# Half tiles moved into the arm that repeats in float32: one branch arm less on the way to the end of an attention and mixture-of-experts kernel

## The chip, the cores and the metric

The kernel runs on one core of one Trainium2 chip. The metric is the time of one execution on the device, in microseconds, as the median of several runs. Lower is better.

## The reference

Attention with capped scores over 4 batches of 12 heads (448 tokens, head size 64), and then a mixture of 8 experts in which each of the 1792 tokens goes to the one expert whose embedding is nearest:

```python
scores = scale * np.matmul(q, k.transpose(0, 1, 3, 2))
scores = cap * np.tanh(scores / cap)
attn = softmax(scores)
x = np.matmul(attn, v)            # (4, 12, 448, 64) -> x: (1792, 768)
...
expert_idx = np.argmax(logits, axis=1)
gate_w = probs[np.arange(N), expert_idx]
for e in range(E):                # E = 8
    mask = expert_idx == e
    h = np.maximum(x[mask] @ w1[e], 0.0)        # w1[e]: 768 x 1024
    out[mask] = gate_w[mask, None] * (h @ w2[e])  # w2[e]: 1024 x 768
```

## The kernel before

The first half of the kernel computes the attention, chooses an expert for each token and counts the tokens of each. After that the experts are ordered by their counts. An expert's place in this order is its position, 0 to 7. Its tokens are taken in tiles of 128. Each weight matrix is split into two float16 halves (`split1`, `split2`), and a product is made of three float16 products. If a sum over the low halves shows that float16 was not enough, the whole mixture is repeated in float32 (`plain_tile`). `fine_sums` and `overflow` compute that test from `sums`: a matmul adds up a count, DVE writes `redo_i`, all engines load it into a register and branch on it (L1575, L1576).

For each position the program holds a number `code` in a register: twice the count of full tiles, plus one if a half tile is left. `position(p)` is nested: `position(p + 1)` stands inside the branch that `position(p)` takes for full tiles. Positions 1 to 4 (`WIDE`) take the leftovers of up to 32 tokens along with a full tile (`wide_tile`) and have no half tiles. From position 5 on there are two branches, one behind the other: `code == 1` runs a half tile (L1547), and `code > 1` runs full tiles and the next position (L1549). Where that second one isn't taken, its `Else` arm asks whether the next position has any tokens (L1555) and runs the half tiles that are left.

`chain(p)` runs the full tiles of one position, with a branch (L1526) ahead of each but the first. `foretell` writes a hint for a branch: it stands some time ahead of the branch and names it and its condition. It is put on TensorE, ScalarE, DVE and POOL, not on SyncE.

`tile_body` (through `any_tile`) is one tile. POOL first computes the tile's `gt` and `idx_out`. TensorE makes the hidden layer in two halves, ScalarE and DVE split each into `hh` and `hl`, and TensorE multiplies by `w2`. Behind the sixth of eight parts it transposes the next tile's `x_tile`, which ScalarE and DVE copy to `xh` and `xl` (`transpose_x`), and POOL scales the one after that (`scale_x`). Then DVE writes `yo`, POOL sends it with an indirect DMA (L677), and POOL gathers one more tile of tokens (L197, L198). The argument `nxt` says which; `False` leaves all of this preparation out. Functions in `hooks` run at numbered places of a tile; 0 to 11 are the steps of its first products.

POOL's program is one queue: indirect DMAs, scalings and the branches stand in order. At the end of the kernel POOL drains and then the engines meet.

Of the kernel before, what the change touches and what calls it, by code (L numbers as in the profile page):

```python
# [30 lines left out]
F32 = mybir.dt.float32  # L31
F32R = mybir.dt.float32r
F16 = mybir.dt.float16
I32 = mybir.dt.int32
AF = mybir.ActivationFunctionType
ALU = mybir.AluOpType
# [44 lines left out]
def attention_moe(ctx: ExitStack, tc: tile.TileContext, q, k, v, cap, emb, tau, w1, w2, qk_pairs, v_pairs, out):  # L81
# [1151 lines left out]
    def positions():  # L1233
# [17 lines left out]
        nc.vector.tensor_copy(pos_i, by_pos[0:1, 3:5, :])  # L1251

    def start_loads():
        for p in range(1, E):
            eid[p] = nc.values_load(
                pos_e[0:1, p : p + 1], engines=(mybir.EngineType.SP,), min_val=0, max_val=E - 1
            )
        for i in range(N1):
            load1(1, i)
        for f in range(N2):  # L1260
            load2(1, f)
# [220 lines left out]
    fine_s = work.tile([P, 1], F16, tag="fine_s", name="fine_s")  # L1482
    redo_i = work.tile([P, 1], I32, tag="redo_i", name="redo_i")

# [5 lines left out]

    def overflow():
        fp = tile_of("h", 0)
        nc.tensor.matmul(fp[:, 0:1], ones16, fine_s, start=True, stop=True)  # L1493
        nc.vector.tensor_scalar(redo_i, fp[:, 0:1], float(P * NF), None, op0=ALU.is_lt)  # L1494


    with tc.manual_schedule():
# [12 lines left out]
        def half_tile(p, hooks=()):  # L1510

            _, base = ends[p]
            any_tile(p, base, base + 3 if p < E - 1 else False, P // 2, hooks=hooks)

# [21 lines left out]
        def position(p):  # L1536
# [10 lines left out]
            with tc.If(code == 1):  # L1547
                half_tile(p, {0: [lambda: foretell(f"full{p}", code > 1)]})
            with tc.If(code > 1, label=f"full{p}") as arm:  # L1549
                chain(p)  # L1550
                position(p + 1)
            if p < E - 1:
                with arm.Else():

                    with tc.If(ends[p + 1][0] > 0):  # L1555
                        for n in range(p + 1, E):
                            with tc.If(ends[n][0] == 1):
                                for f, *a in todo_for(n):
                                    f(*a)
                                half_tile(n)  # L1560

# [9 lines left out]
        fine_sums()  # L1571
        overflow()


        redo = nc.values_load(redo_i[0:1, 0:1], min_val=0, max_val=1)  # L1575
        with tc.If(redo > 0):  # L1576

            nc.vector.tensor_scalar(pos_i[:, 0, :], pos_i[:, 0, :], 1, None, op0=ALU.add)
            nc.vector.tensor_scalar(pos_i[:, 0, :], pos_i[:, 0, :], 1, None, op0=ALU.logical_shift_right)
            nc.vector.tensor_tensor(pos_i[:, 0, 0:1], pos_i[:, 0, 0:1], first_i[0:1, 1:2], op=ALU.add)  # L1580
            nc.vector.memset(pos_i[:, 1, 0:1], 0)
            with tc.For_i(0, E, 1) as p:
                e = nc.values_load(
                    pos_e[0:1, bass.ds(p, 1)], engines=(mybir.EngineType.SP,), min_val=0, max_val=E - 1
                )
                for i in range(N1):
                    nc.sync.dma_start(raw1[i], w1_part(e, i))
                for f in range(N2):
                    nc.sync.dma_start(raw2[f], w2_part(e, f))
                n = nc.values_load(pos_i[0:1, 0, bass.ds(p, 1)], min_val=0, max_val=NT // P + 1)  # L1590
                base = nc.values_load(
                    pos_i[0:1, 1, bass.ds(p, 1)], engines=(mybir.EngineType.Pool,), min_val=0, max_val=TMAX
                )

                with tc.For_i(0, n, 1) as slot:
                    plain_tile(base + slot)
                plain_tile(p + TAIL0)

# [46 lines left out]
```

## Time and profile before

| | |
|---|---|
| median of 3 runs | 546.03 us (545.84 to 549.48) |
| profiled execution | 543.88 us |
| its span, first to last instruction | 542.1 us |
| TensorE busy in the span | 89% |
| DVE, ScalarE, POOL busy | 61%, 55%, 45% |
| mean granted TensorE clock | 0.963 |

Times are in microseconds from the start of the span, unless they are marked ns. The engines are PE (TensorE matmul), PEld (its weight loads), DVE, ACT (ScalarE), POOL and SP; a q behind the name means the sequencer of that engine. Branches, semaphore waits and register loads are the sequencer's work. They are not counted as busy and do not stand in the timeline, but the view of a source line lists them. There a row reads: line, engine, operation and its count, then the shortest, median and longest duration in ns, then the start of the first and of the last. A row of the timeline reads: start, duration, engine, line, operation, tile written and tiles read, shapes, count, and in brackets the idle time before it with what ended it. A row of the stretches gives the stretch, its length, the busy time and count of PE, PEld, DVE, ACT and POOL, the granted clock, the share of the DMA engines and GB/s. The page also lists two DMA queues of the kind "instruction", which carry the program's code to the engines.

### The profile page before, as it was taken

How to read it: one execution, taken by the hardware profiler on the slowest of the kernel's cores; microseconds unless marked ns; L12 is line 12 of the kernel's file. 1: busy time of each engine (PE TensorE's matmuls, PEld its weight loads, DVE VectorE, ACT ScalarE, POOL GpSimd, SP SyncE). 2: the span in 40 equal slices, each digit the busy share in tenths (PEclk: the TensorE clock that was granted, in tenths of full speed). 3: DMA queues.
4: the chain of work that ended last, by engine and by line, in shares of the span. 5: the costliest groups of instructions: out<-in, count | busy, mean ns of one | idle time of the engine just before them, and what ended most of it. 6: DMA issues, size and time to landing. Idle time of an engine off the chain costs nothing. (4 is left out here: it accounts for less than half of the span.)

```text
span 542.1 us, 11950 instructions
## 1 busy us (share of the span) xinstructions
PE 482.8 (89%) x4603; PEld 312.3 (58%) x4604; DVE 329.5 (61%) x712; ACT 300.5 (55%) x371; POOL 245.6 (45%) x294
## 2 busy tenths in 40 slices
PE   3999999999997979979698799999999999998970
PEld 1444444444443434347676578877887788777650
DVE  4876686868698679588719521771125812496710
ACT  3987789788978887926128210831115511567410
POOL 2567556564643454640136412843235623553531
PEclk9999999999999979989999799999999999998995
DMA  7433218331451540325299711491112931297921
GB/s 228 128 112 113 76 63 289 111 112 67 148 207 62 190 160 0 104 73 164 97 390 365 282 40 59 175 344 59 61 60 96 382 114 61 87 366 258 332 86 39
DMA packets 30595, 83.51 MB, mean 154 GB/s; under 512 B 7293, under 2 KB 7449, under 8 KB 30498
## 3 DMA queue, kind: packets, MB, share of 16 engines
q1 hardware_dynamic: 26354, 67.68, 35.7%
q0 software_dynamic: 2896, 13.00, 6.8%
q10 hardware_dynamic: 1248, 1.64, 0.9%
q8 instruction: 47, 0.77, 0.6%
q14 instruction: 50, 0.41, 0.2%
HBM read 69.91 MB, written 13.00 MB: 153 GB/s over the span
## 5 line engine op out<-in xcount | busy, mean ns | idle before, releaser
L780 ACT ACTIVATE prob<-s,icap 128x896 f32<-128x896 f32 x96 | 86.3, 904 | 24.7 <-PE s L774 16.7
L794 POOL TENSOR_TENSOR sums<-sums,prob 128x896 f32<-128x896 f32 x23 | 48.4, 2102 | 81.8 <-DVE sums L792 62.7
L231 PEld LDWEIGHTS <-h 128*128 128x128 f16 x1056 | 79.7, 99 | 7.4 <-issue 3.8
L784 ACT ACTIVATE prob<-prob,cap_b 128x896 f32<-128x896 f32 (+1 forms) x64 | 81.7, 1277 | 2.1
L231 PE MATMUL h<-xh,h 128*128 128x128 f16 (+1 forms) x480 | 78.7, 218 | 2.6 <-ACT x_tile L669 1.4
L231 PE MATMUL h<-xl,h 128*128 128x128 f16 (+1 forms) x480 | 78.8, 218 | 0.9 <-issue 0.9
L231 PE MATMUL h<-xh,l 128*128 128x128 f16 (+1 forms) x480 | 78.8, 218 | 0.5 <-issue 0.4
L811 PE MATMUL v<-prob,vb 128*64 128x448 f32 x288 | 72.2, 581 | 2.9 <-DVE xt L826 2.8
L800 POOL TENSOR_TENSOR sums<-sums,prob 64x448 f32<-64x448 f32 x47 | 64.6, 1375 | 3.6
L204 POOL TENSOR_TENSOR x_tile<-xg 128x768 f32<-128x768 f32 x17 | 25.3, 1489 | 83.8 <-PE xt L212 74.1
L231 PEld LDWEIGHTS <-l 128*128 128x128 f16 x528 | 51.8, 99 | 1.1 <-issue 1.1
L215 ACT CAST xh<-xt 128x384 f16<-128x384 f32 x32 | 13.9, 481 | 68.5 <-PE xt L212 60.5
L244 DVE SCALAR_TENSOR_TENSOR hl<-h,hh 128x512 f16<-128x512 f32 (+1 forms) x20 | 13.3, 664 | 62.6 <-ACT hh L243 62.6
L243 ACT ACTIVATE hh<-h 128x512 f16<-128x512 f32 (+1 forms) x20 | 11.5, 574 | 67.1 <-PE h L231 67.1
L774 PE MATMUL s<-hi 64*128 64x448 f32 x144 | 35.5, 484 | 14.1 <-DVE hi L756 11.8
L1388 PE MATMUL h<-xh,h 128*128 128x160 f16 x192 | 41.1, 237 | 5.1 <-ACTq L1526 2.6
L216 DVE TENSOR_TENSOR xl<-xt,xh 128x384 f16<-128x384 f32 x32 | 16.4, 551 | 46.3 <-ACT xh L215 46.2
L638 PEld LDWEIGHTS <-hh 128*128 128x128 f16 (+1 forms) x352 | 32.9, 100 | 19.4 <-issue 1.2
L222 DVE SCALAR_TENSOR_TENSOR l<-w1r,by_pos,h 128x1024 f16<-128x1024 f32 x30 | 37.7, 1305 | 9.8 <-ACT h L221 9.8
L774 PEld LDWEIGHTS s<-hi 64*128 64x128 f32 x144 | 14.4, 190 | 46.9 <-ACT prob L780 16.0
L1388 PE MATMUL h<-xh,l 128*128 128x160 f16 x192 | 41.1, 238 | 0.0
L1388 PE MATMUL h<-xl,h 128*128 128x160 f16 x192 | 41.0, 237 | 0.0
(312 smaller groups left out, 1132.0 us busy)
## 6 DMA issues: line engine op xcount, KB each, us to landing
w1r<-in_moe_w_dram SPq DMA_DIRECT2D x36, 512.0 KB, 6.8
w2r<-in_moe_w_dram SPq DMA_DIRECT2D x24, 768.0 KB, 7.2
qkb<-in_qk_pairs_dram SPq DMA_DIRECT2D x11, 960.0 KB, 5.1
vb<-in_v_pairs_dram SPq DMA_DIRECT2D x12, 512.0 KB, 5.7
x_dram<-xsb SPq DMA_DIRECT2D x4, 1152.0 KB, 6.5
ring<-in_moe_w_dram SPq DMA_DIRECT2D x6, 512.0 KB, 3.9
ring<-in_moe_w_dram SPq DMA_DIRECT2D x8, 384.0 KB, 3.2
x_dram<-xsb ACTq DMA_DIRECT2D x1, 1152.0 KB
```

The costliest lines, as they stand in the source:

```text
L204: nc.gpsimd.tensor_tensor(x_tile, xg[:, :D], xg[:, SCALE : SCALE + 1].to_broadcast([P, D]), op=ALU.mult)
L216: nc.vector.tensor_tensor(lo, t, hi, op=ALU.subtract)
L222: nc.vector.scalar_tensor_tensor(out=lo, in0=raw, scalar=scale, in1=hi, op0=ALU.mult, op1=ALU.subtract, accum_out=acc)
L231: nc.tensor.matmul(hp[:, f, :W], l[j][:, c], x[:, j, :W], start=j == 0 and f == 0 and n == 0, stop=j == DC - 1 and f == 3 and n == 2, skip ...
L638: nc.tensor.matmul(y, hidden[h][l][:, c, o : o + k], w2p[p % 2][w][f // 2][:, f % 2, m * C : (m + 1) * C], start=f == 0 and n == 0, stop=f ...
L774: nc.tensor.matmul(sp[:, s, :S], l[sl, kc], r[sl, :], start=n == 0, stop=n == 2)
L780: nc.scalar.activation(o, d, AF.Tanh, scale=icap)
L784: nc.scalar.activation(o, o, AF.Exp, scale=cap_b)
L794: nc.gpsimd.tensor_tensor(t, t, pt[:, 4:6, :], op=ALU.add)
L800: eng.tensor_tensor(t[sl, s, :], t[sl, s, :], pt[sl, 6, :], op=ALU.add)
L811: nc.tensor.matmul(o[s * DH : (s + 1) * DH, :S], vb[:, u, s * DH : (s + 1) * DH], pt[:, 2 * u + s, :], start=u == 0, stop=False, skip_grou ...
L1388: nc.tensor.matmul(o, w1p[p % 2][l][j][:, c], x[:, j, :], start=j == 0 and f == fs[0] and m == 0, stop=j == DC - 1 and f == fs[-1] and m == 2,
```

## The change

Five things are changed. `position` loses its `Else` arm, so that the half tiles left at later positions are run inside the arm of the float32 repetition. The condition of that arm, now called `more`, is true if the sums ask for it or if `left`, the count of such half tiles, is above zero; inside, the sums are tested again for the repetition itself. Three small DVE operations in `positions` compute `left`. All half tiles are called with `nxt` False. And a half tile gives a second hint at its place 4: it speaks of the branch `more`, beside the one at its place 0 that speaks of the full tiles.

```diff
@@ positions()
+        a, b = E - WIDE.stop - 1, WIDE.stop + 1
+        two = work.tile([P, 2, a], F32, tag="two", name="two")
+        nc.vector.tensor_scalar(two[:, 0, :], by_pos[:, 3, b - 1 : E - 1], 2.0, None, op0=ALU.is_lt)
+        nc.vector.scalar_tensor_tensor(
+            out=two[:, 1, :], in0=by_pos[:, 3, b:E], scalar=1.0, in1=two[:, 0, :], op0=ALU.is_equal, op1=ALU.mult
+        )
+        nc.vector.tensor_reduce(left, two[:, 1, :], axis=AX.X, op=ALU.add)
...
-    def overflow():
+    def overflow(again):
         fp = tile_of("h", 0)
         nc.tensor.matmul(fp[:, 0:1], ones16, fine_s, start=True, stop=True)
-        nc.vector.tensor_scalar(redo_i, fp[:, 0:1], float(P * NF), None, op0=ALU.is_lt)
+        nc.vector.scalar_tensor_tensor(
+            out=redo_i[:, 0:1], in0=fp[:, 0:1], scalar=float(P * NF), in1=left, op0=ALU.is_lt, op1=ALU.add
+        )
+        if again:
+            nc.vector.tensor_scalar(redo_i[:, 1:2], fp[:, 0:1], float(P * NF), None, op0=ALU.is_lt)
...
         def half_tile(p, hooks=()):
-            _, base = ends[p]
-            any_tile(p, base, base + 3 if p < E - 1 else False, P // 2, hooks=hooks)
+            any_tile(p, ends[p][1], False, P // 2, hooks=hooks)
...
             with tc.If(code == 1):
-                half_tile(p, {0: [lambda: foretell(f"full{p}", code > 1)]})
-            with tc.If(code > 1, label=f"full{p}") as arm:
+                half_tile(p, {0: [lambda: foretell(f"full{p}", code > 1)], 4: [lambda: foretell("more", ends[E - 1][0] > 0)]})
+            with tc.If(code > 1, label=f"full{p}"):
                 chain(p)
                 position(p + 1)
-            if p < E - 1:
-                with arm.Else():
-                    with tc.If(ends[p + 1][0] > 0):
-                        for n in range(p + 1, E):
-                            with tc.If(ends[n][0] == 1):
-                                for f, *a in todo_for(n):
-                                    f(*a)
-                                half_tile(n)
...
         fine_sums()
-        overflow()
-        redo = nc.values_load(redo_i[0:1, 0:1], min_val=0, max_val=1)
-        with tc.If(redo > 0):
-            ...
+        overflow(False)
+        more = nc.values_load(redo_i[0:1, 0:1], min_val=0, max_val=3)
+        with tc.If(more > 0, label="more"):
+            for p in range(WIDE.stop + 1, E):
+                with tc.If(ends[p][0] == 1):
+                    with tc.If(ends[p - 1][0] < 2):
+                        for f, *a in todo_for(p):
+                            f(*a)
+                        transpose_x(*main[1])
+                        scale_x()
+                        half_tile(p)
+            fine_sums()
+            overflow(True)
+            redo = nc.values_load(redo_i[0:1, 1:2], min_val=0, max_val=1)
+            with tc.If(redo > 0):
+                ...
```

## Rows read from the trace of the kernel before

**Rows 1.** The stretches: the last 8.10 us of the span.

```profile
534.00:542.10 8.10, 0.00 (x0) 0.00 (x0) 0.00 (x0) 0.00 (x0) 0.00 (x0) 0.50 0.03 7
```

**Rows 2.** Timeline of POOL from 505 us on.

```profile
526.68 0.18 POOL L620 COPY gt<-gt 64x1 f32<-64x1 f32 x1
...
527.13 1.47 POOL L204 TENSOR_TENSOR x_tile<-xg 128x768 f32<-128x768 f32 x1
...
528.88 1.10 POOL L677 DMA_INDIRECT out_dram<-yo,idx_out  x1 [0.15 <-issue]
...
530.47 1.06 POOL L198 DMA_INDIRECT xg<-x_dram,idx_in  x1 [0.28 <-POOL idx_in L197]
```

**Rows 3.** Timeline of DVE from 505 us on.

```profile
507.60 1.82 DVE L222 SCALAR_TENSOR_TENSOR l<-w2r,by_pos,h 128x1536 f16<-128x1536 f32 x1 [2.64 <-issue]
...
526.90 0.62 DVE L675 TENSOR_SCALAR yo<-y,gt 128x384 f32<-128x384 f32 x1 [0.44 <-POOL gt L620]
532.71 0.28 DVE L1486 TENSOR_TENSOR fine<-sums 128x111 f32<-128x111 f32 x1 [5.19 <-DVEq L1555]
...
533.82 0.16 DVE L1494 TENSOR_SCALAR redo_i<-h 128x1 int32<-128x1 f32 x1 [0.28 <-PE h L1493]
```

**Rows 4.** Source line L1549, all engines.

```profile
L1549 PEldq COMPARE_BRANCH  x1: 451/451/451, 524.6 to 524.6; - x1
...
L1549 DVEq COMPARE_BRANCH  x1: 80/80/80, 527.4 to 527.4; - x1
L1549 POOLq COMPARE_BRANCH  x1: 67/67/67, 530.8 to 530.8; - x1
```

**Rows 5.** Source line L1555, all engines.

```profile
L1555 PEldq COMPARE_BRANCH  x2: 196/2476/4757, 525.1 to 530.1; - x2
...
L1555 DVEq COMPARE_BRANCH  x2: 54/62/70, 529.9 to 532.5; - x2
L1555 POOLq COMPARE_BRANCH  x2: 43/47/51, 533.2 to 535.7; - x2
...
L1555 POOLq INC_SWDGE_SEM  x1: 952/952/952, 533.6 to 533.6; - x1
```

**Rows 6.** Source line L1576, all engines.

```profile
L1576 POOLq EVENT_SEMAPHORE  x4: 17/17/43, 536.8 to 537.0; - x4
...
L1576 DVEq EVENT_SEMAPHORE  x2: 21/21/21, 535.5 to 535.6; - x2
...
L1576 DVEq COMPARE_BRANCH  x1: 56/56/56, 534.4 to 534.4; - x1
L1576 PEldq COMPARE_BRANCH  x1: 3968/3968/3968, 534.4 to 534.4; - x1
...
L1576 POOLq COMPARE_BRANCH  x1: 50/50/50, 536.3 to 536.3; - x1
L1576 POOLq INC_SWDGE_SEM  x1: 928/928/928, 537.1 to 537.1; - x1
```

**Rows 7.** Source line L1641 on POOL, 536 to 545 us.

```profile
L1641 POOLq DRAIN  x3: 46/117/3174, 538.1 to 541.8; - x3
```

**Rows 8.** Source line L1526, all engines.

```profile
L1526 DVEq COMPARE_BRANCH  x15: 43/47/92, 308.1 to 514.1; - x15
...
L1526 DVEq EVENT_SEMAPHORE  x5: 21/21/21, 341.7 to 514.7; - x5
```

**Rows 9.** Source line L1526 on POOL, 505 to 545 us.

```profile
L1526 POOLq EVENT_SEMAPHORE  x5: 17/43/1200, 522.7 to 523.0; - x5
...
L1526 POOLq COMPARE_BRANCH  x1: 64/64/64, 519.5 to 519.5; - x1
```

**Rows 10.** Timeline of DVE from 269 to 276 us.

```profile
270.68 0.16 DVE L1251 CAST pos_i<-by_pos 1x16 int32<-1x16 f32 x1
274.36 0.69 DVE L244 SCALAR_TENSOR_TENSOR hl<-h,hh 128x512 f16<-128x512 f32 x1 [3.52 <-ACT hh L243]
```

**Rows 11.** DMA issues from 500 us on, KB, median us to landing.

```profile
out_dram<-yo,idx_out POOLq DMA_INDIRECT x2, 3.2
```

More of the change, by code (lines that the diff above doesn't have):

```diff
@@ L1482, in attention_moe @@
     fine_s = work.tile([P, 1], F16, tag="fine_s", name="fine_s")
-    redo_i = work.tile([P, 1], I32, tag="redo_i", name="redo_i")
+    redo_i = work.tile([P, 2], I32, tag="redo_i", name="redo_i")
+    left = work.tile([P, 1], F32, name="left")
     def fine_sums():
@@ L1571, in attention_moe @@
         fine_sums()
-        overflow()
-        redo = nc.values_load(redo_i[0:1, 0:1], min_val=0, max_val=1)
-        with tc.If(redo > 0):
[L1578 to L1597, printed above, removed]
@@ new lines, in attention_moe @@
+        overflow(False)
[13 more added lines that the diff above has]
+            with tc.If(redo > 0):
+                nc.vector.tensor_scalar(pos_i[:, 0, :], pos_i[:, 0, :], 1, None, op0=ALU.add)
+                nc.vector.tensor_scalar(pos_i[:, 0, :], pos_i[:, 0, :], 1, None, op0=ALU.logical_shift_right)
+                nc.vector.tensor_tensor(pos_i[:, 0, 0:1], pos_i[:, 0, 0:1], first_i[0:1, 1:2], op=ALU.add)
+                nc.vector.memset(pos_i[:, 1, 0:1], 0)
+                with tc.For_i(0, E, 1) as p:
+                    e = nc.values_load(
+                        pos_e[0:1, bass.ds(p, 1)], engines=(mybir.EngineType.SP,), min_val=0, max_val=E - 1
+                    )
+                    for i in range(N1):
+                        nc.sync.dma_start(raw1[i], w1_part(e, i))
+                    for f in range(N2):
+                        nc.sync.dma_start(raw2[f], w2_part(e, f))
+                    n = nc.values_load(pos_i[0:1, 0, bass.ds(p, 1)], min_val=0, max_val=NT // P + 1)
+                    base = nc.values_load(
+                        pos_i[0:1, 1, bass.ds(p, 1)], engines=(mybir.EngineType.Pool,), min_val=0, max_val=TMAX
+                    )
+                    with tc.For_i(0, n, 1) as slot:
+                        plain_tile(base + slot)
+                    plain_tile(p + TAIL0)
```

## The prediction

> **What bounds the kernel now.** TensorE is busy for 89% of the span, but the change doesn't touch the tiles where it works. It touches one half tile, at position 5, and what comes behind it. So I read the end of the trace first: the table of stretches, then the timelines of POOL and DVE from 505 us on, and last, because branches aren't counted as busy, the view of each source line that branches there (L1549, L1555, L1576), which lists the sequencers' own instructions. The reader is to see that no engine computes in the last 8.10 us [rows 1], and that the 15 us from the half tile's last output on are a chain of branches.
>
> Four things stand on that chain. First, DVE writes the half tile's `yo` at 526.90, released by POOL's `gt`, not by TensorE [rows 2, 3]; it ends at 527.52. Second, POOL doesn't send it at once: the next tile's `x_tile` (1.47 us), which nobody uses, stands ahead, and the output goes at 528.88; a gather that nobody uses follows at 530.47 [rows 2]. Third, each engine jumps twice. L1549 jumps over the full tiles of positions 5 to 7 into the `Else` arm, and the branch there, L1555, jumps over the half tiles in that arm. On DVE L1549 stands at 527.4 and the next instruction, L1555, at 529.9; the one after that (its second L1555) at 532.5 [rows 4, 5]. So two jumps cost 5 us in which DVE waits for nothing but code, and `fine` starts at 532.71 [rows 3]. POOL pays 2.4 us once, from L1549 at 530.8 to L1555 at 533.2, then an increment of a DMA semaphore at L1555 (952 ns) and a like one at L1549, and leaves at 535.7 [rows 4, 5]. Fourth, the test itself: `redo_i` is ready at 533.98 [rows 3], but POOL takes its branch L1576 only at 536.3, because it was late. Then come a third increment (928 ns), a drain of 3.17 us from 538.1 on, and closing semaphores to the span's end at 542.1 [rows 6, 7]. TensorE's jump at L1576 is longer (3.97 us from 534.4 [rows 6]), but it ends at 538.4, three microseconds ahead of the end of POOL's drain. POOL's chain sets the end.
>
> **The change part by part.** I sum along POOL.
>
> The three small DVE operations behind `pos_i` cost nothing: DVE has nothing to do for 3.52 us there, until ScalarE's `hh` releases it at 274.36, and three operations like L1251's 0.16 us, one behind the other, take some 0.6 [rows 10]. If that cover were gone, 0.6 us would be the price.
>
> *No scaling of a next tile.* `x_tile` goes, and with it `gates`. The output then waits for `yo` alone, and goes at 527.55 instead of 528.88: -1.3 us. The six transposes, two copies and two subtractions that go on TensorE, ScalarE and DVE bring nothing, since `yo` waits for `gt`, and that for POOL's late end of position 4.
>
> *No gather.* Between the output and L1549 POOL now spends 1.9 us (528.88 to 530.8 [rows 2, 4]) on the index copy and the issue of the gather. Without them the branch can follow the output as it now follows the gather, 0.3 us behind its start, or wait for the issue of the output (1.1 us) to end. So the gain is between 0.8 and 1.6, even 1.9 if the sequencer runs ahead of the output; I take 1.3.
>
> *One jump instead of two, and one arm less to leave.* L1549 stays, now over the full tiles alone, and I leave its 2.4 us as they are: the same hint was given before, in the same place, and POOL and DVE paid all the same. What goes is L1555. On DVE it is worth 2.4 us: L1549 at 527.4, landing at 529.9, `fine` at 530.2, `redo_i` at 531.5 (both at the distances of [rows 3]). On POOL no second jump was paid; what it saves there is one increment of the two and its semaphores, 1.1 us (0 if both stay, 1.2 at most). POOL then is ready for `more` at 535.7 - 1.3 - 1.3 - 1.1 = 532.0, still behind `redo_i` at 531.5, so POOL goes on setting the end, by half a microsecond. Half of what DVE gains is therefore lost.
>
> *The last jump.* It went over the float32 repetition; now it goes over two half tiles with their splits as well. Its price isn't in the trace. POOL paid 0.4 at L1576 (536.3 to the first semaphore at 536.8), DVE 1.1 (534.4 to 535.5) [rows 6], and a jump to code that wasn't there cost 2.4 on either. So it is between 0.4 and 2.4 on POOL; I take DVE's 1.1, since the distance grows, but a hint now speaks of it, given one branch earlier: +0.7. The branches from the new landing place to the test can cross into code that isn't there either: 0 to 0.9, taken as 0. The hints themselves add two short instructions to each of four engines, beside running work.
>
> *Unchanged:* the last increment, the drain, the closing semaphores. I have no reason for the drain's length in the trace, so I carry all 3.17 us along.
>
> Sum: -1.3 - 1.3 - 1.1 + 0.7 = -3.0 us. The profiled execution took 543.88 us with a span of 542.1; the median of the runs shown is 546.03 (545.84 to 549.48). Nothing in the change touches the difference, so I take the saving off the median: 543.0. TensorE's last jump, even at the 4.76 us of its longest [rows 5], would start at 531.9 and end at 536.7, while POOL's drain would end at 538.3: not late.
>
> The Trainium skill ("Runtime: NRT & Kernel Launch", section "Instruction fetch mechanics") says that code is loaded ahead purely in sequence, and that a taken branch to code outside the window stops the engine until a load from memory. The gaps of POOL and DVE behind L1549 agree, with 2.4 us each, although a hint had been given. TensorE doesn't: its hinted L1549 took 0.45 us, its unhinted L1555 4.76 [rows 4, 5]. By the rule alone the hints buy nothing; that is the second rival.
>
> **The rivals.**
>
> *Both hints reach all engines.* DVE does show cheap far branches: at the end of position 4, L1526 at 514.1 is followed at 514.7 (the last of five such ends) [rows 8]. Then L1549 saves POOL up to 1.9 more and the last jump costs 0.4. But POOL's semaphores wait for the output's landing, 3.2 us behind its issue [rows 11], so not before 530.8, and with an increment POOL is ready at 531.7: only 0.3 earlier than forecast. With the 0.7 that is -4.0, and with the largest values of the other terms -4.9: 541.1 to 542.0. Against it: at 519.5 POOL took a hinted branch and went on at 522.7 [rows 9], and the half tile puts the hint just ahead of its branch on POOL.
>
> *No hint helps, and the last jump is paid in full.* For it speaks the same row of POOL, and L1549 on POOL and DVE. Then the last jump costs POOL 2.4, or 2.0 more than now: -1.3 - 1.3 - 1.1 + 2.0 = -1.7, that is 544.3; with the 0.9 for a crossing 545.2.
>
> *Slower: the moved code.* The three operations stand in DVE's program ahead of all of positions 1 to 7, so that every later place where DVE's code must be loaded falls a few instructions earlier. One such place shows: at 507.60 DVE stood still for 2.64 us with nothing to wait for but its issue [rows 3]. Two new stalls of that kind, where TensorE waits for a split or `hl`, cost 5.3 us and turn -3.0 into +2.3: 548.3. It decides from the second stall on; one leaves the change at about zero. Against it: nothing of the kind shows at the last of the five ends on DVE [rows 8], and the shift is small.
>
> *The change doesn't do what it says:* one told branch displaces the other. TensorE would then pay 4.8 at L1549 and be there at 529.4, ahead of `fine_s`. It would not show in the time.
>
> **How the numbers follow.** The forecast (541.8 to 543.9) has 0.50, both hints 0.15, no hint 0.25, moved code 0.07, with 0.03 for what I haven't thought of. The likeliest gives 543.0. The terms at their best (-1.3, -1.9, -1.2, 0, with a little for the landing) reach -4.9, at their worst (-1.3, -0.8, 0, +2.0, +0.9) +0.8; I put the range at 540.6 to 546.2, which leaves out most of the moved code. One per cent, 5.5 us, is about what a measurement of this kernel can tell from no change: 0.09 faster by more, 0.87 within, 0.04 slower by more.
>
> **What would show it.** In the profile after: the output of the half tile goes within 0.1 us of the end of `yo`; no `x_tile` behind it; on DVE one gap of 2.4 us instead of two, and `fine` at about 530.2; POOL with one increment less, at its load of `redo_i` by about 532; the span near 539. If POOL passes L1549 without a gap, the hint works and I am too high. If the gap behind the last branch on POOL is over 2 us, I am too low. If the drain shrinks or grows with its surroundings, the whole end moves by it, and that term was never understood. If DVE stands still in new places before 515 us, the third rival has it.

## The result and the profile after

The kernel after took 542.7 us (median of 6 runs), the kernel before, run beside it, 546.6 (6 runs). The ratio is 0.991, with a 95% interval of 0.9881 to 0.9939: 4.9 us less, between 3.3 and 6.5. The medians lie 3.9 us apart; the ratio, which is the measure here, leaves out the one slow run of after, at 550.4 us. The prediction said 543.0 and a saving of 3.0. The number was met and the saving is larger than its sum. The profiled execution of after took 543.00 us with a span of 541.3, only 0.8 less than the span of before, so this pair of traces alone would mislead. It has to be read stage by stage, and a stage of one trace is one execution, while a ratio is made of several.

What the prediction spoke of is the end behind `yo`. Timelines of POOL and of DVE in the kernel after, answering to [rows 2, 3]:

```profile
528.53 0.18 POOL L620 COPY gt<-gt 64x1 f32<-64x1 f32 x1
529.77 1.10 POOL L677 DMA_INDIRECT out_dram<-yo,idx_out  x1 [1.05 <-DVE yo L675]
```

```profile
528.87 0.62 DVE L675 TENSOR_SCALAR yo<-y,gt 128x384 f32<-128x384 f32 x1 [2.99 <-PE y L638]
532.73 0.28 DVE L1495 TENSOR_TENSOR fine<-sums 128x111 f32<-128x111 f32 x1 [3.24 <-DVEq L1562]
...
533.83 0.16 DVE L1504 SCALAR_TENSOR_TENSOR redo_i<-h,left 128x1 int32<-128x1 f32 x1 [0.27 <-PE h L1502]
```

The output goes 0.90 us behind the start of `yo` (1.98 before), no `x_tile` and no gather follow, and `fine` starts 3.9 us behind `yo` (5.8 before), since DVE stands still once and not twice. L1562 of after is L1549 of before, the branch over the full tiles. Here is its source line in after, answering to [rows 4, 5] (x2 counts the branch at the end of the `If` too; duration as least, median, largest in ns, then the starts of the first and the last):

```profile
L1562 POOLq EVENT_SEMAPHORE  x5: 17/43/43, 532.7 to 533.8; - x5
...
L1562 PEldq COMPARE_BRANCH  x2: 202/1841/3480, 527.1 to 530.8; - x2
L1562 DVEq COMPARE_BRANCH  x2: 68/114/159, 529.3 to 532.4; - x2
L1562 POOLq COMPARE_BRANCH  x2: 54/90/125, 529.9 to 534.8; - x2
...
L1562 POOLq INC_SWDGE_SEM  x1: 918/918/918, 533.9 to 533.9; - x1
```

TensorE, which passed this branch in 0.45 us before, now pays 3.48. POOL branches at 529.9 and lands at 532.7: 2.8 us, where L1549 took 2.4 before. It has one increment instead of two. But its five semaphores stretch over 1.1 us (532.7 to 533.8), where the two of L1555 took 0.1 before. The last branch, L1580, which was L1576 in [rows 6], and the drain of [rows 7]:

```profile
L1580 POOLq EVENT_SEMAPHORE  x5: 17/17/43, 536.0 to 536.4; - x5
...
L1580 DVEq EVENT_SEMAPHORE  x2: 21/21/21, 535.0 to 535.1; - x2
...
L1580 DVEq COMPARE_BRANCH  x1: 85/85/85, 534.4 to 534.4; - x1
L1580 PEldq COMPARE_BRANCH  x1: 463/463/463, 534.4 to 534.4; - x1
...
L1580 POOLq COMPARE_BRANCH  x1: 68/68/68, 535.5 to 535.5; - x1
```

```profile
L1659 POOLq DRAIN  x3: 46/113/3092, 537.4 to 541.0; - x3
```

TensorE's last jump fell from 3.97 us to 0.46, POOL's stayed at 0.5, the drain at 3.1. From the start of `yo` to the end of the span it is 12.4 us instead of 15.2.

Two stages ahead of `yo` differ as well. Timeline of TensorE in before: the first matmul of position 4, the first of the half tile, and the one behind its first gap; then the same three in after:

```profile
491.04 0.23 PE L1388 MATMUL h<-xh,h 128*128 128x160 f16 x1 [2.51 <-PEq L1526]
...
514.96 0.19 PE L231 MATMUL h<-xh,h 128*128 128x64 f16 x1 [0.76 <-ACTq L1526]
...
516.01 0.19 PE L231 MATMUL h<-xh,l 128*128 128x64 f16 x1 [0.39 <-issue]
```

```profile
493.56 0.23 PE L1396 MATMUL h<-xh,h 128*128 128x160 f16 x1 [2.54 <-PEq L1539]
...
515.10 0.19 PE L231 MATMUL h<-xh,h 128*128 128x64 f16 x1 [0.76 <-ACTq L1539]
...
518.58 0.21 PE L231 MATMUL h<-xh,l 128*128 128x64 f16 x1 [2.82 <-issue]
```

Position 4 takes 21.5 us in after and 23.9 in before. The half tile, from its first matmul to `yo`, takes 13.8 and 11.9. TensorE pauses in it for 2.82 us with nothing to wait for, but that alone doesn't make it longer: `yo` also needs POOL's `gt`, which ends at 528.71, 13.6 us into the half tile (11.9 in before) and only 0.16 ahead of `yo`. POOL is late from its second output of position 4 on. Timelines of POOL in before and in after:

```profile
518.27 0.98 POOL L1447 DMA_INDIRECT out_dram<-yo,idx_out  x1 [2.99 <-ACT hh L243]
```

```profile
519.90 0.98 POOL L1455 DMA_INDIRECT out_dram<-yo,idx_out  x1 [4.68 <-DMA out_dram<-yo_a,idx_a]
```

In after this output waits until the one ahead of it has landed, and goes 4.8 us behind the half tile's first matmul, against 3.3 in before. The three stages give -2.4, +1.8 and -2.8. Ahead of them after's trace is 2.5 us behind (position 4 starts at 493.56 and not at 491.04). That is no sign of the change: in a second trace of the same kernel, a_again below, it starts at 492.05, and in all fourteen traces between 490.2 and 494.9. The change's own place is the last stage, and whether the other two belong to it is what the experiments had to settle.

### The profile page after: what moved, and what is told of

Same layout as the page of the kernel before. It is cut to its first block, busy times and chain, and to the rows that moved or that the text cites. A ratio compares the mean times of both kernels' runs of the same rounds, so it can differ in the third digit from the quotient of the medians.

```text
span 541.3 us, 11929 instructions
## 1 busy us (share of the span) xinstructions
PE 479.0 (88%) x4597; PEld 311.6 (58%) x4598; DVE 335.4 (62%) x713; ACT 299.7 (55%) x369; POOL 239.2 (44%) x289
## 5 line engine op out<-in xcount | busy, mean ns | idle before, releaser
L231 PEld LDWEIGHTS <-h 128*128 128x128 f16 x1056 | 81.5, 100 | 10.3 <-issue 6.6
L811 PE MATMUL v<-prob,vb 128*64 128x448 f32 x288 | 70.0, 565 | 3.0 <-DVE xt L826 2.9
L204 POOL TENSOR_TENSOR x_tile<-xg 128x768 f32<-128x768 f32 x16 | 23.5, 1467 | 82.8 <-PE xt L212 72.9
L244 DVE SCALAR_TENSOR_TENSOR hl<-h,hh 128x512 f16<-128x512 f32 (+1 forms) x20 | 13.3, 664 | 65.3 <-ACT hh L243 65.3
L231 PEld LDWEIGHTS <-l 128*128 128x128 f16 x528 | 52.9, 100 | 0.8 <-issue 0.8
L774 PE MATMUL s<-hi 64*128 64x448 f32 x144 | 34.8, 475 | 15.3 <-DVE hi L756 12.8
L1396 PE MATMUL h<-xh,h 128*128 128x160 f16 x192 | 39.9, 233 | 5.2 <-ACTq L1539 2.6
L774 PEld LDWEIGHTS s<-hi 64*128 64x128 f32 x144 | 14.1, 188 | 47.7 <-ACT prob L780 18.9
L638 PE MATMUL y<-h,hl 128*128 128x384 f16 (+1 forms) x160 | 38.2, 329 | 2.0 <-DVE hl L244 2.0
L1396 PE MATMUL h<-xh,l 128*128 128x160 f16 x192 | 39.9, 233 | 0.0
```

The lines of the kernel that those rows point to most:

```text
L204: nc.gpsimd.tensor_tensor(x_tile, xg[:, :D], xg[:, SCALE : SCALE + 1].to_broadcast([P, D]), op=ALU.mult)
L231: nc.tensor.matmul(hp[:, f, :W], l[j][:, c], x[:, j, :W], start=j == 0 and f == 0 and n == 0, stop=j == DC - 1 and f == 3 and n == 2, skip ...
L638: nc.tensor.matmul(y, hidden[h][l][:, c, o : o + k], w2p[p % 2][w][f // 2][:, f % 2, m * C : (m + 1) * C], start=f == 0 and n == 0, stop=f ...
L774: nc.tensor.matmul(sp[:, s, :S], l[sl, kc], r[sl, :], start=n == 0, stop=n == 2)
L811: nc.tensor.matmul(o[s * DH : (s + 1) * DH, :S], vb[:, u, s * DH : (s + 1) * DH], pt[:, 2 * u + s, :], start=u == 0, stop=False, skip_grou ...
L1396: nc.tensor.matmul(o, w1p[p % 2][l][j][:, c], x[:, j, :], start=j == 0 and f == fs[0] and m == 0, stop=j == DC - 1 and f == fs[-1] and m == 2,
```

## The experiments

Every run gave a trace, and each trace is read by the same three stages: position 4 (first matmul to the half tile's first), half tile (to the start of `yo`), behind `yo` (to the end of the span). Ratios are against the kernel before, run beside each.

| kernel | position 4 | half tile | behind yo | sum | ratio (95% interval) |
|---|---|---|---|---|---|
| before | 23.9 | 11.9 | 15.2 | 51.1 | |
| after | 21.5 | 13.8 | 12.4 | 47.7 | 0.991 (0.9881 to 0.9939) |
| a_again | 21.6 | 13.9 | 12.9 | 48.4 | 0.9917 (0.9883 to 0.995) |
| b_noprep | 23.9 | 13.4 | 13.3 | 50.5 | 0.9959 (0.9932 to 0.9987) |
| a_prep | 21.5 | 14.6 | 17.2 | 53.3 | 1.0004 (0.9973 to 1.0035) |
| a_onehint | 23.0 | 12.9 | 14.1 | 50.1 | 0.9972 (0.995 to 0.9993) |
| b_ops | 21.5 | 13.4 | 15.3 | 50.2 | 0.9982 (0.9957 to 1.0007) |
| a_noops | 23.7 | 12.5 | 13.0 | 49.1 | 0.9959 (0.9938 to 0.998) |
| a_onlymore | 23.2 | 11.3 | 12.8 | 47.2 | 0.9954 (0.9929 to 0.9979) |
| b_behind | 23.2 | 14.1 | 15.1 | 52.4 | 1.0022 (0.9986 to 1.0058) |
| a_pad | 21.5 | 13.5 | 12.2 | 47.2 | 0.9931 (0.9897 to 0.9965) |
| v_late | 23.0 | 12.6 | 14.2 | 49.8 | 0.9968 (0.9939 to 0.9997) |
| v_early | 23.2 | 13.3 | 12.1 | 48.6 | 0.9928 (0.9904 to 0.9952) |
| v_best | 21.5 | 13.5 | 12.1 | 47.1 | 0.9927 (0.9898 to 0.9956) |

The stages have to be read together. Against before, their sum in one trace and the ratio agree within 2.1 us. Position 4 and the half tile together take 35.3 us on the mean of the six traces with the shortest position 4, and 36.4 on that of the three with the longest, where position 4 alone differs by 2.1 to 2.4. So the half tile takes back about half of what position 4 gains. There `gt` ends 13.0 to 13.9 us behind the first matmul in the six, and 11.9 to 13.3 in the three. The landing that POOL waits for took 5.3 us in a_again and 3.9 in a_onlymore, where the half tile is the shortest of all, though TensorE pauses in it for 1.96 us. Why the landing differs wasn't tried.

### The preparation alone, and all but it

b_noprep is the kernel before with half tiles that prepare nothing. Its arm prepares each half tile itself, as in after.

```diff
-            any_tile(p, base, base + 3 if p < E - 1 else False, P // 2, hooks=hooks)
+            any_tile(p, ends[p][1], False, P // 2, hooks=hooks)
```

> The kernel before, with one part of the change: half tiles prepare no next tile. Theory (the steps as summed along POOL, 3 us shorter in all): the output goes right behind yo and L1549 is reached some 2.6 us sooner on POOL, but DVE still pays both jumps, so redo_i is not ready sooner than 7 us behind yo, and POOL, which left for its load 9 us behind yo, now waits for it. Behind yo the span gets 1.7 to 1.9 us shorter, not 2.6; time about 1.8 us below the kernel before. Rival A (the removed preparation is the whole gain): as fast as the kernel after, 3.5 to 4 us below before. Rival B (the gain came from where code happens to be loaded, in the tiles ahead): within 0.5 us of before. TensorE's pause of 2.8 us inside the half tile, which the trace of after has and that of before (0.39) doesn't: if it is a matter of the run, it may show here; if the change makes it, it doesn't.

Measured: 0.9959, 2.2 us below before, and 13.3 us behind `yo`, 1.9 less. The theory's reason shows in the trace. Timeline of DVE in b_noprep, and its line L1576, the load of `redo_i` (L1575 before):

```profile
528.85 0.62 DVE L675 TENSOR_SCALAR yo<-y,gt 128x384 f32<-128x384 f32 x1 [4.39 <-POOL gt L620]
...
535.81 0.16 DVE L1494 TENSOR_SCALAR redo_i<-h 128x1 int32<-128x1 f32 x1 [0.28 <-PE h L1493]
```

```profile
L1576 POOLq TENSOR_LOAD <-redo_i x1: 337/337/337, 536.0 to 536.0; - x1
```

POOL's load stands at 536.0, right behind the end of `redo_i` at 535.97. DVE with its two jumps has become the bound, and part of POOL's gain is lost. The pause of TensorE in the half tile is there too (1.75 us), with this one part of the change alone.

a_prep is the kernel after with the preparation put back:

```diff
-            any_tile(p, ends[p][1], False, P // 2, hooks=hooks)
+            any_tile(p, base, base + 3 if prepare else False, P // 2, hooks=hooks)
```

> The kernel after, with the preparation of a next tile put back into the half tile (scaling, transposes, gather). Theory: the output goes 1.3 us behind yo again and POOL reaches its branch some 2.6 us later, with one arm and one increment less than before: 2.0 to 2.6 us above the kernel after, 1.1 to 1.9 below before. Rival A (the removed preparation is the whole gain): as slow as before. Rival B (the gain came from the code's place in the tiles ahead): as fast as after, within 0.5 us. If TensorE's pause of 2.8 us in the half tile comes with the new order of the code, it shows here again; if with the missing preparation, not.

Measured: 1.0004, as slow as before and some 5 us above after; 17.2 us behind `yo`. In time that is what rival A says, but not for its reason: position 4 stays at 21.5 us, and the end behind `yo` is 2.0 us longer than that of before. The theory's 2.0 to 2.6 was too small, and one of its terms didn't come: the output goes 0.9 us behind `yo`, as in after, since here `yo` itself is late, 1.3 us behind `gt`. Two of the missing microseconds and more are code that POOL waits for at places where after has it. Lines L1563 (the branch over the full tiles), L1580 and L1581 (load and last branch) in a_prep:

```profile
L1563 POOLq COMPARE_BRANCH  x2: 54/90/125, 530.5 to 535.8; - x2
```

```profile
L1580 POOLq TENSOR_LOAD <-redo_i x1: 327/327/327, 537.5 to 537.5; - x1
```

```profile
L1581 POOLq EVENT_SEMAPHORE  x5: 17/17/43, 539.7 to 540.0; - x5
...
L1581 POOLq COMPARE_BRANCH  x1: 68/68/68, 537.9 to 537.9; - x1
```

From the branch at 535.8 to the load it is 1.7 us (0.3 in after), and the last jump takes 1.8 (0.5 in after), although it was told. Why the longer half tile has these two wasn't tried.

### The second hint

a_onehint is after without it:

```diff
-                half_tile(p, {0: [...], 4: [lambda: foretell("more", ends[E - 1][0] > 0)]})
+                half_tile(p, {0: [...]})
```

> The kernel after without its second hint (the one that tells of the arm). Theory: TensorE's hinted jump over the full tiles falls back from 3.48 us to about 0.45, and its jump over the arm rises from 0.46 to about 4; DVE's last jump goes from 0.5 to 1.0; neither ends last, so the time stays within 0.7 us of after. Rival (the hint is what made POOL's last jump 0.4 us): POOL pays 2.4 there and the time is 2 us above after. TensorE's pause of 2.8 us in the half tile stands ahead of the second hint; if it stays, that hint is not its cause.

Measured: 0.9972, some 3 us above after. The theory falls and its rival holds, at a higher price. TensorE's first jump did go back to 0.44 us, and its last one rose to 4.25, but that isn't what counts. Line L1580, the last branch, in a_onehint:

```profile
L1580 POOLq EVENT_SEMAPHORE  x5: 17/17/43, 539.2 to 539.6; - x5
...
L1580 DVEq EVENT_SEMAPHORE  x2: 21/21/21, 539.2 to 539.3; - x2
...
L1580 DVEq COMPARE_BRANCH  x1: 64/64/64, 535.5 to 535.5; - x1
L1580 PEldq COMPARE_BRANCH  x1: 4248/4248/4248, 535.5 to 535.5; - x1
...
L1580 POOLq COMPARE_BRANCH  x1: 56/56/56, 535.9 to 535.9; - x1
```

POOL branches at 535.9 and lands at 539.2: 3.3 us, against 0.5 with the hint. DVE pays 3.7. The hint takes this price away. That it is the longer arm that made the jump dear (0.5 us on POOL in before, without a hint) is argued, not tried. The end behind `yo` is 14.1 us, 1.2 to 1.7 above after; position 4 is 1.4 longer (23.0), of which below, and the half tile 0.8 to 1.0 shorter, so the trace doesn't account for all of the 3 us.

a_onlymore is after without the first hint:

```diff
-                half_tile(p, {0: [lambda: foretell(f"full{p}", code > 1)], 4: [...]})
+                half_tile(p, {4: [...]})
```

> The kernel after without its first hint (over the full tiles); the second, of the arm, stays. Theory (on each engine the later hint takes the place of the earlier, so the first has no effect left): L1562 costs 2.8 us on POOL and DVE and 3.5 to 4.8 on TensorE as in after, POOL's last jump 0.5, and the time is within 0.7 us of after. Rival A (the first hint helps somewhere ahead of the branch): 1 us or more above after. Rival B (the two hints together cause the 0.8 us which POOL stands between the first two semaphores behind L1562; with one hint alone that was 0.1): POOL lands without it and the time is 0.8 us below after.

In the trace the first hint does nothing in after: without it L1562 costs TensorE 3.42 us, POOL 2.8 and DVE 3.0, and the end behind `yo` is 12.8 us. The 0.8 us between POOL's semaphores didn't go, so rival B is wrong. The time, 0.9954, is 2.0 us above a_again, more than the theory's 0.7, but the intervals overlap, and the trace doesn't show the difference: position 4 is 1.6 us longer (23.2 against 21.6) and the half tile 2.6 shorter (11.3 against 13.9).

v_late gives the second hint behind the landing of L1562:

```diff
         position(1)
+        foretell("more", ends[E - 1][0] > 0)
         fine_sums()
```

> The kernel after with its second hint (of the arm) given behind the jump over the full tiles, ahead of fine, 2.7 us ahead of POOL's last branch, instead of in the half tile. Theory A (a hint takes effect only when its engine next enters new code): POOL enters none between the hint and the branch, so its last jump costs 3.4 us again, the first one 2.3 without the 0.8 to 1.2 us between its first two semaphores; TensorE's first jump falls to 0.45 us; the end behind yo is 14.1 us as with one hint alone. Theory B (a hint acts at once): POOL's last jump costs 0.5, the end behind yo about 11.6, 0.8 us below that of after. In both position 4 takes 21.6 or 23.2 us, as ScalarE's stall has it.

As theory A says: 14.2 us behind `yo`, a ratio of 0.9968, and the last jump paid in full. Lines L1660 (where the hints stand) and L1581 (the last branch) in v_late:

```profile
L1660 PEldq BRANCH_PREFETCH_HINT  x1: 40/40/40, 530.8 to 530.8; - x1
L1660 DVEq BRANCH_PREFETCH_HINT  x1: 38/38/38, 533.9 to 533.9; - x1
```

```profile
L1581 POOLq EVENT_SEMAPHORE  x5: 17/17/43, 539.3 to 539.7; - x5
...
L1581 PEldq COMPARE_BRANCH  x1: 4323/4323/4323, 535.7 to 535.7; - x1
...
L1581 POOLq COMPARE_BRANCH  x1: 59/59/59, 536.0 to 536.0; - x1
```

TensorE had the hint 4.9 us ahead of the branch and still paid 4.32. On POOL it came only 0.5 us ahead, not the 2.7 that was expected, so POOL's 3.3 us here tell little.

### The first hint, given earlier

v_early tells ScalarE, DVE and POOL of the jump over the full tiles in the tile of position 4:

```diff
-                    foretell(f"more{p}_1", code > 3)
+                    foretell(f"more{p}_1", code > 3, TOLD[:1] if p == WIDE.stop - 1 else TOLD)
+                    if p == WIDE.stop - 1:
+                        foretell(f"full{p + 1}", ends[p + 1][0] > 1, TOLD[1:])
```

> The kernel after with the first hint moved: ScalarE, DVE and POOL are told of the jump over the full tiles in the tile of position 4, ahead of the branch that ends it, in place of the hint that told them of that branch; TensorE keeps its hint in the half tile, and only the other three are told of the arm there. Theory (a hint takes effect when its engine next enters new code, and DVE and POOL enter none between the hint and the branch in the half tile): L1562 falls to 0.5 us on DVE and POOL; POOL's increment then waits for the output's landing, 3.2 us behind its issue, so the end behind yo gets about 0.9 us shorter; the branch at the end of position 4 costs DVE and ScalarE 2.4 us, in a wait. 0.9 us below after. Rival A (a hint lasts only up to the next branch): L1562 stays at 2.8, the time is that of after. Rival B (the lost hints of position 4 delay the start of the half tile): 1 us or more above after.

The jump is as the theory says. Line L1569, the same branch, in v_early:

```profile
L1569 POOLq EVENT_SEMAPHORE  x5: 17/43/43, 530.4 to 533.0; - x5
...
L1569 DVEq COMPARE_BRANCH  x2: 75/102/129, 529.2 to 530.1; - x2
L1569 POOLq COMPARE_BRANCH  x2: 60/78/95, 529.7 to 534.1; - x2
...
L1569 DVEq EVENT_SEMAPHORE  x1: 21/21/21, 530.0 to 530.0; - x1
```

DVE lands after 0.8 us instead of 3.0, POOL after 0.6 instead of 2.8. The branch at the end of position 4 didn't cost DVE the 2.4 us that were expected (0.6, as in after). And POOL gains little: its semaphores stand from 530.4 to 533.0, because it waits for the landing of the output. That landing in the views of the DMA issues of v_early and of a_again (last number: us from issue to landing):

```profile
out_dram<-yo,idx_out POOLq DMA_INDIRECT x1, 3.3
```

```profile
out_dram<-yo,idx_out POOLq DMA_INDIRECT x1, 4.1
```

Issued at 529.45 it lands at 532.8 in v_early; issued at 528.50 at 532.6 in a_again, where POOL's five semaphores last from 531.4 to 532.9. The views list this landing in five traces, also in a_onlymore (4.0), a_noops (4.3) and v_best (3.3), and in each the last of POOL's five semaphores stands 0.2 to 0.3 us behind it. So the 1.1 us in which they stretch in after, where the landing isn't listed, are the same wait. The end behind `yo` is 12.1 us, 0.3 to 0.7 below after, while position 4 is 1.6 longer; the time, 0.9928, is that of after and not 0.9 below it.

### The three operations, and where code lies

b_ops is the kernel before with only the three operations behind `pos_i`; b_behind has them in the float32 repetition instead, which isn't entered; a_noops is after without them:

```diff
+        nc.vector.tensor_scalar(two[:, 0, :], by_pos[:, 3, b - 1 : E - 1], 2.0, None, op0=ALU.is_lt)
+        nc.vector.scalar_tensor_tensor(
+            out=two[:, 1, :], in0=by_pos[:, 3, b:E], scalar=1.0, in1=two[:, 0, :], op0=ALU.is_equal, op1=ALU.mult
+        )
+        nc.vector.tensor_reduce(left, two[:, 1, :], axis=AX.X, op=ALU.add)
```

> The kernel before, with only the three small DVE operations behind pos_i added (their result is used by nobody). Theory: they run inside a wait of 3.5 us, so the time is that of before within 0.5 us, and everything behind yo is unchanged. Rival (moved code): they shift all later code of DVE; the stall of 2.64 us at DVE's splits in position 4 (507.6 in the trace of before, gone in that of after) goes or moves, and the time falls by up to 2 us, or rises by as much if another stall comes where TensorE waits.

> The kernel after without the three DVE operations; the test is made on the overflow alone, so half tiles left over would not be noticed (there are none with these inputs). Theory (these operations shift DVE's later code, and that is why its 2.6 us stall at the splits of position 4 is gone): the stall is back, position 4 takes 23.9 us again, and the time is 1 to 2.4 us above after; the end behind yo stays at 12.4. Rival (the stall has gone for another reason, or is covered): position 4 stays at 21.5 us and the time within 0.5 us of after.

> The kernel before with the three DVE operations added at the end, in the float32 repetition, which isn't entered: the same program length as with them behind pos_i, but nothing ahead of position 4 is moved within DVE's program. Theory (DVE's stall in position 4 goes because the operations move the code behind them): the stall of 2.6 us is there, position 4 takes 23.6 to 23.9 us, and the time is that of before within 0.7 us. Rival (the length of the program decides, or the place of the whole): the stall is gone, position 4 takes 21.5 us and the time is 1 to 2.4 us below before.

Timelines of DVE at the same two splits of position 4, in b_ops, a_noops and b_behind; [rows 3] has the second of them for before:

```profile
505.88 1.81 DVE L222 SCALAR_TENSOR_TENSOR l<-w2r,by_pos,h 128x1536 f16<-128x1536 f32 x1
...
507.62 1.81 DVE L222 SCALAR_TENSOR_TENSOR l<-w2r,by_pos,h 128x1536 f16<-128x1536 f32 x1
```

```profile
509.30 1.82 DVE L222 SCALAR_TENSOR_TENSOR l<-w2r,by_pos,h 128x1536 f16<-128x1536 f32 x1 [2.53 <-issue]
```

```profile
509.43 1.82 DVE L222 SCALAR_TENSOR_TENSOR l<-w2r,by_pos,h 128x1536 f16<-128x1536 f32 x1 [2.95 <-issue]
```

The stall of 2.5 to 2.95 us is there in all four kernels without the operations ahead of it (before, b_noprep, a_noops, b_behind) and in none of the ten that have them there. Behind the splits they don't remove it. So it is DVE's code moved by three instructions, and nothing that they compute. The times fit but don't separate theory and rival by themselves: 1.0 us between before and b_ops (from a gain of 2.4 to a loss of 0.4), 2.3 between a_noops and a_again (about 2 either way, an estimate from the two intervals), and b_behind 1.2 above before (from 0.8 below to 3.2 above). Nor is this the price of DVE's stall alone, as the next stall shows.

ScalarE has a stall of its own at its first `hh` of position 4: 1.5 to 1.65 us in before, b_noprep, a_noops, a_onehint, a_onlymore, v_early and v_late, none in the others. b_ops and after have lost it as well, so the 1.0 and the 2.3 us are of both stalls. Timelines of ScalarE in b_noprep and in b_behind:

```profile
497.23 0.57 ACT L1400 ACTIVATE hh<-h 128x480 f16<-128x480 f32 x1 [1.65 <-issue]
```

```profile
497.61 0.57 ACT L1400 ACTIVATE hh<-h 128x480 f16<-128x480 f32 x1
```

b_behind differs from before only in three DVE instructions that are never run (and in two small tiles), and ScalarE's stall is gone, in one trace of each. With both stalls position 4 takes 23.7 to 23.9 us, with one 23.0 to 23.2, with none 21.5 to 21.6. So a_onehint, a_onlymore and v_early are longer in position 4 by ScalarE's stall, of which the half tile gives a part back. v_best, which is v_early with the program length of after, and a_pad, which is after with one more hint of each engine in the arm that isn't entered, were to test this:

```diff
+            foretell("redo", redo > 0)
-            with tc.If(redo > 0):
+            with tc.If(redo > 0, label="redo"):
```

> v_early, with one hint of each engine added in code that isn't entered with these inputs (ahead of the inner test of the arm) and the hints of the half tiles of positions 6 and 7, not entered either, given back, so that every engine's program has as many instructions as in after. Theory (in v_early the end behind yo is 12.1 us against 12.4 to 12.9, but ScalarE stood still for 1.65 us at its first hh of position 4, which after doesn't show; whether it does depends on where the code lies, also of code that is never run): with the old length the stall is gone, position 4 takes 21.6 us instead of 23.2, the end behind yo stays at 12.1, and the time is 0.5 to 1 us below after, some 5.5 us below before. Rival (the moved hint itself makes ScalarE's stall): position 4 stays at 23.2 us and the time within 0.7 us of v_early, 4 us below before.

> The kernel after with one hint of each engine added in the arm that isn't entered, ahead of its inner test. Nothing that runs is changed. Theory (ScalarE's stall in position 4 depends on the length of code that is never run): the stall of 1.5 to 1.65 us may show, and then position 4 takes 23.2 us instead of 21.6 and the time is 1.5 us above after. Rival (only the hints that run matter): no stall, position 4 takes 21.6 us, the time is that of after within 0.5 us.

v_best has lost the stall (`hh` at 494.19, right behind the split ahead of it) with code that isn't run, position 4 takes 21.5 us and the end 12.1. That is the theory's trace, but not its time: 0.9927, 4.0 us below before (2.4 to 5.6), where the theory said 5.5, so no version here is shown to beat the kernel after. a_pad shows no stall, which both sides allowed. Which lengths bring ScalarE's stall stays open, and with one kernel alone traced twice (after and a_again, neither with it), so does whether it can come and go between executions.

> The kernel after, unchanged, for a second trace of it and as the measure for the three kernels beside it. Theory: what differs from the kernel before is the end behind yo (12.4 us against 15.2 to 15.3) and position 4 (21.5 us from its first matmul to that of the half tile, against 23.9); both must show again, and the time is 4 to 5 us below before. The pause of TensorE inside the half tile (1.75 to 2.82 us in five traces of both kinds, 0.39 in the first trace of before alone) belongs to neither kernel: it shows again. Rival (the tail was a lucky run): the end behind yo is 13.5 us or more.

a_again, the kernel after once more, repeats both differences (21.6 and 12.9 us) and the pause in the half tile (2.57).

## Why the prediction was right, point by point

Behind `yo` the account is right in the main: -3.0 forecast, -2.8 and -2.3 measured (after and a_again). That the sum came out is in part luck, since one term was 1.2 us too hopeful and two others 0.5 and 0.6 too careful. So, in part, is the number, 543.0: the gain in position 4 is missing from its sum, and the base of 546.03 was 0.6 below the 546.6 that the kernel before took in the runs beside after.

**The output right behind `yo`, forecast -1.3.** -1.1 in after, -1.0 in a_again: it goes 0.3 us behind the end of `yo`, not within 0.1, since POOL takes the branch L1560 in between.

**No gather, forecast -1.3 within -0.8 to -1.9.** -1.8: POOL branches 0.1 us behind the start of its output, near the end of the range at which the sequencer runs ahead of the output.

**One jump and one increment less, forecast -1.1 on POOL.** This is the term that failed. From its branch to the load of `redo_i` POOL took 5.1 us in before, 5.2 in after and 5.6 in a_again: +0.1 and +0.5. The increment did go, and DVE gained most of what was said (`fine` at 3.9 behind `yo`, forecast 3.3). But POOL now waits for the output to land, 3.3 us behind the issue in v_early and 4.1 in a_again. From its branch to the start of its increment it is 4.0 us in after and 2.8 in before (to L1555's), 1.2 more, as much as the other increment gave. The jump in it, whose 2.4 us the prediction left as they are, takes 2.8 (2.3 in a_onehint and v_late, where the second hint isn't given ahead of it), but that is covered by the wait. The prediction knew this wait, put it at 3.2 and used it only in its first rival. With the queue emptied ahead of it, it is what is late next, and v_early shows it alone: there the jump is cheap and the end still comes only 0.3 to 0.7 us sooner.

**The last jump, forecast +0.7 within 0 to +2.0.** +0.1 with the hint. Without it (a_onehint) the jump cost 3.3 us, beyond the upper bound of 2.4, so the second rival would have been dearer than it said. The prediction had the reason in one clause, that a hint given one branch earlier speaks of it, and gave it too little weight.

**Drain and closing** gave -0.1. The four terms and this make -2.8 in after and -2.3 in a_again, against -3.0.

**The three operations, forecast at nothing.** They hide as said (`hl` still waits 2.21 us for ScalarE behind them in after), but they move DVE's code, and that took away a stall of 2.64 us which the prediction had in front of it [rows 3]. It asked in its third rival only for new stalls, at +5.3 us. The mechanism was right and the sign wasn't: a stall that is there can vanish as well as one can come. This, with ScalarE's stall, is 1.0 to 2.3 us in time, and the part of the saving that the sum lacks. Without the operations (a_noops) the saving is 2.2 us.

**The base.** The saving was taken off the median 546.03 and not off the profiled 543.88. That came out better: taken off the profiled time, the forecast would have been 540.9. The reason is not shown. The trace of before is the only one of fourteen in which TensorE doesn't pause in the half tile (0.39 us against 1.75 to 2.82). It pauses in b_ops and b_noprep as well, and in b_behind, which runs what before runs, so the change isn't needed for the pause. Whether it is a matter of the execution or of where the code lies stays open, since before has one trace.

**One hint displaces the other.** This rival held on TensorE (3.48 us at L1562, 0.44 with the first hint alone), and as it said, TensorE's loss doesn't show in the time: TensorE is through at 530.8, and `fine_s` comes at 533.3. It holds in small on DVE too, which is on the way to `fine`: 3.0 us at L1562, and 2.4 with the first hint alone.

The Trainium skill ("Runtime: NRT & Kernel Launch", section "Instruction fetch mechanics") says that code is loaded ahead purely in sequence and that a taken branch out of the loaded window stalls the engine. The untold jumps agree (3.3 us on POOL in a_onehint). The told ones don't: 0.5 us for the same jump in after, 0.6 in v_early against 2.8. Here the measurement decides.

## What to carry to other kernels

When work ahead of a wait is removed, price the wait that stands behind it in the same queue before counting the gain; here an output's landing took back what a removed increment gave. A small edit moves code, and on engines that stall for code a stall can go as well as come, so look for the ones that are there, and compare kernels over several executions and stage by stage, not by one pair of traces. By the reading of hints below, tell an engine of a jump before it enters the code that holds the branch, one hint at a time, and check on that engine's own line whether it lands sooner.

## What was not expected of the hardware

A hint far ahead of its branch can do nothing. In a_onehint DVE was told 13.6 us ahead and paid 2.4, as much as for the untold L1555 in before (2.5); TensorE in v_late was told 4.9 us ahead and paid 4.32. Told one branch earlier, DVE and POOL paid 0.8 and 0.6. All runs fit the reading that a hint acts when its engine next moves into other code, and that of two given before that the later one counts; the first part is argued from these runs, not shown by itself.

Code that is never run seems to change what the engines pay in code that is: with three more DVE instructions at the end of the program ScalarE's stall of 1.65 us in position 4 was gone (one trace of each).

Behind its pause of 2.82 us in the half tile TensorE's clock falls to half in after. Table of stretches in after (columns: stretch, its length, busy time and instructions of TensorE's matmuls, weight loads, DVE, ScalarE, POOL, then the granted clock, the DMA share, GB/s):

```profile
514.00:516.00 2.00, 0.99 (x20) 0.66 (x18) 0.62 (x1) 0.58 (x1) 1.10 (x1) 1.00 1.04 398
516.00:518.00 2.00, 0.00 (x0) 0.00 (x0) 0.00 (x0) 0.00 (x0) 0.00 (x0) 0.72 0.47 163
518.00:520.00 2.00, 1.42 (x28) 1.42 (x28) 0.00 (x0) 0.00 (x0) 0.10 (x1) 0.50 0.05 13
...
522.00:524.00 2.00, 2.00 (x47) 2.00 (x45) 0.43 (x2) 0.38 (x1) 0.42 (x1) 0.58 0.63 176
524.00:526.00 2.00, 2.00 (x43) 1.56 (x41) 0.59 (x3) 0.38 (x1) 0.00 (x0) 1.00 0.37 114
```

No matmul ran from 516 to 518, the granted clock went from 1.00 (2.4 GHz) to 0.50 (1.2 GHz), and it came back within 522 to 524. By this trace `yo` was at most 0.16 us later for the pause and the clock, because it also has to wait for POOL's `gt`, until 528.71. And the pause doesn't always cost clock. a_pad, which runs the same instructions, has no matmul from 516 to 518 either:

```profile
516.00:518.00 2.00, 0.00 (x0) 0.00 (x0) 0.00 (x0) 0.00 (x0) 0.00 (x0) 1.00 0.38 132
518.00:520.00 2.00, 1.88 (x65) 1.88 (x65) 0.00 (x0) 0.00 (x0) 0.51 (x1) 1.00 0.04 8
```

There the granted clock stays at 1.00, behind a pause of 2.37 us, and in v_early it falls to 0.50 behind one of 1.97. What decides it isn't shown. a_pad's half tile, at full clock, takes 13.5 us, only 0.3 less than after's: `yo` goes right behind `gt`, which ends 13.5 us behind the first matmul there.
